# Spectral layer with a feed-forward gate: the second chunk transposed by DMA behind six tiles of w1, and each of these tiles scaled alone

## The chip, the cores and the metric

The kernel runs on one core of a Trainium2 chip. The core's engines work side by side, each through its own list of instructions in order: TensorE (PE in the profile: matmuls, and transposes as matmuls with an identity), VectorE (DVE), ScalarE (ACT), GpSimd (POOL) and SyncE (SP, which here only issues DMAs). They wait for one another by semaphores. Tiles stand in SBUF (128 partitions); matmuls write PSUM. The metric is the device time of one execution in microseconds (us); lower is better.

## What is computed

```python
def reference(A_x, A_w_r, A_w_i, B_x, B_w1, B_w2):
    x = A_x                                   # 1 x 2048 x 1024
    xn = _layernorm(x, axis=-1)
    X = rfft2(xn) * (w_r + 1j * w_i)          # over the last two axes
    s = irfft2(X, s=(2048, 1024))
    h = silu(einsum("bsd,df->bsf", xn, B_w1)) # B_w1: 1024 x 3584
    g = silu(einsum("bsf,fd->bsd", h, B_w2))  # B_w2: 3584 x 1024
    return x + s * g
```

## The kernel before

All matmuls take fp16. A float32 operand is scaled by a power of two and split into a high half (rounded to fp16) and a low half (the rest), and a product is three passes: high by high, high by low, low by high.

*Rows.* The 2048 rows stand in four chunks c = 0 to 3 of 512, each in four parts p of 128. `ln_gen(c)` normalises a chunk: statistics of a part on VectorE (L701 to 704), three small steps on POOL (L706 to 708), the normalisation on ScalarE (L709). Chunks 0 and 1 are then transposed on TensorE into `tp` (L718), ScalarE rounds the high half out of PSUM (L722, tile xnT) and VectorE takes the low half (L726). Chunks 2 and 3 (`TURNED`) are normalised into `xp` (two buffers), ScalarE takes the high half into `xs` (L687), VectorE the low half (L680), and both are transposed into xnT by DMAs on SP (L673), two per part. `xs` is one tile with room for a whole chunk (tag V, one buffer): the next chunk's `xs` may be written only when all DMA transposes of the one before have been read out.

*w1.* It is used in 28 tiles f of 128 columns. Of each: load (L271, SP), maximum of the absolute values per row (L274, VectorE), a column sum by one small matmul with ones (L258, TensorE, tile `s`), a chain of four small steps on VectorE that makes a power of two (`e`, `r`, `rs`; L279 to 282), the high half on ScalarE (L251), the low half on VectorE (L254). In the start two tiles share one column sum and one chain.

*First layer.* Product (c, f), `mm1`, is 24 matmuls (eight blocks d of the inner dimension by three passes) into one of four PSUM banks `pa`. For the first product the eight high-by-high matmuls come first; in the others the three passes of a block stand together. ScalarE evacuates it with silu into `h32` (L465), one tile for two f and two chunks, with two buffers. When its four parts are there, `hidden` forms sums and differences for the second layer, which is done with seven instead of eight block products: `hr` on VectorE (L494, L495), then high halves on ScalarE (`hosum`, `hoone`, L251), low halves on VectorE (L254), and seven stores to DRAM on SP (`hd_...`, L488). `hosum` and `hoone` have one buffer each: the next pair's high half waits until the stores of the one before have landed.

*Transforms.* `fa_mat` (L782 to 784) transforms a part of a chunk along the columns, 24 matmuls with 128 columns; ScalarE takes it out (L791, L792) and VectorE does the butterflies (L802 to 847). Later stages give s; `iu` and `ub` belong to the inverse transform, far behind.

*Order.* The program records instructions in a hand-written order; each engine executes its part of that list. The loop over `order` records product after product, and between products it takes steps ("slots") from two queues of generators: `bg` (normalisation, transforms) and `wq` (w1 tiles). `defer` puts DMA issues some steps later. Before the first product a list `WARM` alternates steps of the queues with spins, matmuls on ones whose result is not used (L1465). `FILL` names products with a transform block ahead of them; `EXTRA` names places with one more `wq` step.

## Time and profile before

| | us |
|---|---|
| median of three runs | 1235.21 (1234.19 to 1236.31) |
| the profiled execution | 1235.84 |
| its span | 1234.1 |
| TensorE busy in it | 1220.7 |
| VectorE / ScalarE / POOL busy | 999.0 / 467.6 / 117.3 |

The profile was taken in one execution. Its span runs from the first to the last instruction on the engines; the time of the same execution is 1.7 us longer. Rows name engine, line, output and inputs by the program's names without their numbers (pa for pa0_3), and give shapes as partitions by elements. In a timeline the first two columns are start and duration in us; brackets show idle time of that engine before, and what ended it. In a group's row stand busy time in all and nanoseconds of one, then idle time before. In a waits row stand total, count and longest. A row of windows has the stretch, its length, busy time of PE, PEld (weight loads), DVE, ACT and POOL with counts, the granted TensorE clock (1.00 is full speed), the DMA engines' share, and GB/s.

### The profile page before, as it was taken

What the parts mean: (1) busy time and instruction counts of PE and PEld (TensorE: products, weight loads), DVE (VectorE), ACT (ScalarE), POOL (GpSimd) and SP (SyncE); (2) the same over time, 40 slices, a digit from 0 to 9 for tenths busy, and PEclk for the clock granted to TensorE, in tenths of its full rate; (3) what the DMA queues carried; (4) which work ended last, traced back from release to release, by engine and by line L of the source; (5) the groups of instructions that cost most, each with busy time, mean ns of one, the idle gap of its engine ahead of it and who ended that gap; (6) DMA issues with size and microseconds to landing.
All of it is one profiled execution on the core that took longest, in us unless ns stands there. A gap on an engine that the chain in (4) does not pass through costs nothing.

```text
span 1234.1 us, 19097 instructions
## 1 busy us (share of the span) xinstructions
PE 1220.7 (99%) x7033; PEld 625.2 (51%) x7033; DVE 999.0 (81%) x1970; ACT 467.6 (38%) x614; POOL 117.3 (10%) x245
## 2 busy tenths in 40 slices
PE   8999999999999999999999999999999999999998
PEld 5545445444544454445545555554455555555545
DVE  7687988899798898896969899985186678798886
ACT  4865344333554565444433222122032222243212
POOL 2330000001000000010001121114111111000000
PEclk9999999999999999999999999999999999999999
DMA  7487476655758898759898999997989999998576
GB/s 253 134 172 187 135 224 201 185 152 161 223 172 237 276 283 242 217 177 279 207 283 224 283 259 198 276 256 246 293 207 278 286 289 331 315 332 325 200 261 260
DMA packets 271102, 293.67 MB, mean 238 GB/s; under 512 B 40096, under 2 KB 198816, under 8 KB 270624
## 3 DMA queue, kind: packets, MB, share of 16 engines
q1 hardware_dynamic: 250992, 233.66, 65.7%
q10 hardware_dynamic: 15984, 51.45, 12.0%
q0 software_dynamic: 4032, 7.34, 3.5%
q8 instruction: 55, 0.90, 0.3%
q14 instruction: 39, 0.32, 0.1%
HBM read 185.95 MB, written 102.25 MB: 234 GB/s over the span
## 4 chain that ended last, share of the span: by engine, by line
PE 75%; DVE 11%; DMA 9%; issue 2%; ACT 1%; SPq 0%; POOL 0%; DVEq 0%; ACTq 0%; POOLq 0%
PE pa L456 45%; PE pb L539 8%; PE pb L541 8%; PE pb L540 8%; DVE Z L1055 2%; DMA wq<-in_A_w_i_dram 2%; DMA sd<-s 2%; PE id L1294 2%; DMA zd<-zq 1%; DMA ht<-hd_sum_d 1%; DVE T L1020 1%; DVE w L254 1%; PE iu L1204 1%; ACT xp L709 1%; PE iu L1212 1%
## 5 line engine op out<-in xcount | busy, mean ns | idle before, releaser
L456 PE MATMUL pa<-xnT,w 128*128 128x512 f16 x2688 | 585.2, 379 | 1.1 <-ACT w L251 0.7
L456 PEld LDWEIGHTS <-w 128*128 128x128 f16 x2688 | 262.2, 98 | 311.6 <-DVE w L254 1.3
L539 PE MATMUL pb<-w,ht 128*128 128x512 f16 (+2 forms) x812 | 300.4, 372 | 0.0
L540 PE MATMUL pb<-w,ht 128*128 128x512 f16 (+2 forms) x812 | 300.4, 372 | 0.0
L541 PE MATMUL pb<-w,ht 128*128 128x512 f16 (+2 forms) x812 | 300.3, 372 | 0.0
L541 PEld LDWEIGHTS <-ht 128*128 128x128 f16 x812 | 79.4, 98 | 91.0
L539 PEld LDWEIGHTS <-ht 128*128 128x128 f16 x812 | 79.5, 98 | 86.7
L540 PEld LDWEIGHTS <-ht 128*128 128x128 f16 x812 | 79.4, 98 | 86.7
L465 ACT ACTIVATE h<-pa,s 128x512 f32<-128x512 f32 x112 | 75.5, 678 | 122.9 <-PE pa L456 111.0
L251 ACT ACTIVATE w<-jr,sc 128x512 f16<-128x512 f32 x98 | 68.1, 713 | 77.8 <-PE pb L541 22.1
L254 DVE SCALAR_TENSOR_TENSOR w<-jr,sc,w 128x512 f16<-128x512 f32 x98 | 71.1, 744 | 2.1 <-ACT w L251 2.1
L254 DVE SCALAR_TENSOR_TENSOR hoone<-h,hs,hoone 128x2048 f16<-128x2048 f32 x28 | 65.6, 2344 | 7.9 <-ACT hoone L251 7.9
L251 ACT ACTIVATE hoone<-h,hs 128x2048 f16<-128x2048 f32 x28 | 56.0, 1998 | 36.5 <-DVE h L499 24.3
L251 ACT ACTIVATE hosum<-hr,hs 128x1536 f16<-128x1536 f32 x28 | 44.1, 1574 | 64.1 <-DVE hr L495 26.8
L981 ACT ACTIVATE zq<-Z,zs 128x1024 f16<-128x1024 f32 x16 | 18.4, 1149 | 103.9 <-DVE Z L1055 57.0
L494 DVE TENSOR_TENSOR hr<-h 128x1024 f32<-128x1024 f32 x28 | 34.2, 1221 | 24.4 <-ACT h L465 24.3
L254 DVE SCALAR_TENSOR_TENSOR hosum<-hr,hs,hosum 128x1536 f16<-128x1536 f32 x28 | 50.7, 1812 | 3.1 <-ACT hosum L251 3.1
L251 ACT ACTIVATE w<-w1r,rs 128x1024 f16<-128x1024 f32 x28 | 31.9, 1144 | 47.0 <-DVE w L254 31.8
L274 DVE TENSOR_REDUCE m<-w1r 128x1 f32<-128x1024 f32 x28 | 33.8, 1210 | 16.1 <-DMA w1r<-in_B_w_dram 16.1
L632 ACT ACTIVATE pl<-pl,c 128x512 f32<-128x512 f32 (+2 forms) x28 | 17.6, 657 | 70.1 <-DVE pl L608 41.6
L954 PE MATMUL fx<-vq,kq 128*128 128x256 f16 x192 | 43.2, 273 | 0.0
L955 PE MATMUL fx<-vq,kq 128*128 128x128 f16 x192 | 42.0, 219 | 0.0
(219 smaller groups left out, 1524.8 us busy)
## 6 DMA issues: line engine op xcount, KB each, us to landing
w1r<-in_B_w_dram SPq DMA_DIRECT2D x28, 512.0 KB, 6.2
hd_sum<-hosum SPq DMA_DIRECT2D x56, 256.0 KB, 2.9
hd_one<-hoone SPq DMA_DIRECT2D x56, 256.0 KB, 3.7
hd_dif<-hoone SPq DMA_DIRECT2D x56, 256.0 KB, 3.2
w2m<-in_B_w_dram SPq DMA_DIRECT2D x28, 512.0 KB, 5.2
ht<-hd_dif ACTq DMA_DIRECT2D x32, 448.0 KB, 6.3
jr<-in_B_w_dram SPq DMA_DIRECT2D x56, 256.0 KB, 6.8
ht<-hd_sum ACTq DMA_DIRECT2D x32, 448.0 KB, 6.4
```

The lines of the kernel that those rows point to most:

```text
L251: nc.scalar.activation(hi, raw, AF.Copy, scale=scale)
L254: nc.vector.scalar_tensor_tensor(lo, raw, scale, hi, op0=OP.mult, op1=OP.subtract)
L274: nc.vector.tensor_reduce(m1[:, i:i + 1], raw[i], axis=AX.XY, op=OP.max, apply_absolute_value=True)
L456: nc.tensor.matmul(ps, w[:, wh, d], xt[:, xh, d], start=(n == 0), stop=(n == 23))
L465: nc.scalar.activation(hq[:, 2 * (c % 2) + f % 2], ps, AF.Silu, scale=s1[:, f:f + 1])
L494: tt(sums[:, 0:2], hq[:, 0::2], hq[:, 1::2], op=OP.subtract)
L539: nc.tensor.matmul(ps, hh[:, 0], w[:, 0], start=first, stop=False)
L540: nc.tensor.matmul(ps, hh[:, 0], w[:, 1], start=False, stop=False)
L541: nc.tensor.matmul(ps, hh[:, 1], w[:, 0], start=False, stop=last)
L954: nc.tensor.matmul(o, k[:, c, kh, 1], v[:, c, vh], start=(n == 0), stop=False)
L955: nc.tensor.matmul(ps[:, c, 0], k[:, c, kh, 2], v[:, c, vh, 128:256], start=False, stop=False)
L1055: eng.tensor_tensor(Z[:, ns, pos], x0[:, :, ls], x1[:, :, ls], op=o_)
```

## The change

The order of the first twelve products becomes chunk 0 with f = 0 to 5, then chunk 1 with f = 0 to 5; before it was chunk 0 and 1 with f = 0 to 3, then both with 4 and 5. Chunk 1 is no longer transposed on TensorE: a new generator `entering` normalises it into `xp`, splits it and transposes it by DMA, as chunks 2 and 3 are; 32 transposes on TensorE go and eight on SP come. The first six tiles of w1 are scaled one by one (a sum and chain each), in a list of 24 steps; the high half of tile 0 is made on VectorE, and tile 1's maximum on ScalarE as a sum over |w| (`AF.Abs` with `accum_out`). Tiles 4 and 5 are loaded earlier, the next chunk's x later. In products with f up to 5 and c up to 1 all high-by-high matmuls come first. During the first six products, steps of the queues are recorded inside a product, after its 8th and 16th matmul and after its end (`ENTRY`: w and b are steps of the queues, f and e a transform block and its evacuation). Products (0, 4) and (0, 5) are evacuated into a tile `h32_early` and copied into their `h32` tile when (1, 4) is evacuated. The spins become 61 from 71. A line number of before moves by 1 to 30 in the changed file.

```diff
@@ -19,13 +19,14 @@
 S, D, F, DF = 2048, 1024, 3584, 513
 NFT = F // 128
 NP = NFT // 2
-WARM = [35, 8, 0, 8, 0, 8, 12, 0, 0, 0, 0]
+WARM = ("", 35), ("b", 10), ("w", 0), ("b", 0), ("w", 8), ("w", 0), ("b", 8), ("w", 0), ("b", 0), ("w", 0)
 LEAD, PAUSE, LAST, EARLY = 1.0, -1, 6, 2
 IORDER = (1, 3, 0, 2)
 SUMMED = (4, 5)
 TURNED = (2, 3)
-FILL = ((1, 0), (3, 0))
-EXTRA = (4, 5, 6, 7, 20, 22, 24)
+FILL = ((1, 0),)
+EXTRA = (20, 22, 24)
+ENTRY = ("wwbb|w|w", "ww|bbwb|", "fww|b|wbbwwb", "wbwb||w", "wbwbww|b|b", "be|b|bb")
 
 
 
@@ -300,28 +301,32 @@
         for i in range(4):
             load(i)
         yield 0
-        maxi(0)
-        yield 0
-        maxi(1)
-        yield 0
-        scales(0, 2)
-        yield 0
-        split(0)
-        yield 0
-        rest(0)
-        yield 0
-        split(1)
-        rest(1)
-        maxi(2)
-        maxi(3)
-        yield 0
-        scales(2, 2)
-        split(2)
-        rest(2)
-        yield 2
-        split(3)
-        rest(3)
-        yield 2
+        def whole(i):
+
+            if i == 0:
+                new[0] = fp.tile([128, 2, 8, 128], F16, name="w1_0", tag="w1", bufs=7)
+                nc.vector.tensor_single_scalar(new[0][:, 0], raw[0], rs[:, 0:1], op=OP.mult)
+            else:
+                split(i)
+            if i in (1, 2):
+                load(i + 3)
+
+        def bound(i):
+
+            if i == 1:
+                junk = A["p"].tile([128, 8, 128], F16, name="w1abs", tag="junk", bufs=1)
+                nc.scalar.activation(junk, raw[1], AF.Abs, accum_out=m1[:, 1:2])
+            else:
+                maxi(i)
+
+        def scale(i):
+            scales(i, 1)
+
+        steps = {"m": bound, "s": scale, "h": whole, "l": rest}
+        for k in "m0 s0 h0 m1 l0 s1 h1 m2 l1 s2 h2 m3 l2 s3 h3 l3 m4 s4 h4 m5 l4 s5 h5 l5".split():
+            steps[k[0]](int(k[1]))
+            yield 0
+
         def ahead(i):
 
             if i < NFT and i not in raw and i - len(used1) <= 4:
@@ -329,7 +334,7 @@
                 load(i + 1)
 
         last = None
-        for i in range(4, NFT, 2):
+        for i in range(6, NFT, 2):
             while i not in raw:
                 ahead(i)
                 yield 0
@@ -446,21 +451,30 @@
 
     done2, ready2, chunks = [0], [-1], [0]
 
-    def mm1(c, f):
+    def mm1(c, f, between={}):
         ps = pf.tile([128, 512], F32, name=f"pa{c}_{f}", tag="ff")
         w, xt = w1t[f], xnT[c]
         terms = [(d, wh, xh) for wh, xh in ((0, 0), (0, 1), (1, 0)) for d in range(8)]
-        if c + f:
+        if f > 5 or c > 1:
             terms.sort(key=lambda k: k[0])
         for n, (d, wh, xh) in enumerate(terms):
+            if n in between:
+                between[n]()
             nc.tensor.matmul(ps, w[:, wh, d], xt[:, xh, d], start=(n == 0), stop=(n == 23))
         if c == 3:
             used1.add(f)
         q, g = f // 2, c // 2
 
         def evac():
+            if (q, c) == (2, 0):
+                if f % 2 == 0:
+                    h32["early"] = A["p"].tile([128, 2, 512], F32, name="h32_early", tag="Ro", bufs=1)
+                nc.scalar.activation(h32["early"][:, f % 2], ps, AF.Silu, scale=s1[:, f:f + 1])
+                return None
             if (q, g) not in h32:
                 h32[q, g] = H["p"].tile([128, 4, 512], F32, name=f"h32_{q}_{g}", tag="h32", bufs=2)
+                if (q, c) == (2, 1):
+                    nc.scalar.activation(h32[q, g][:, 0:2], h32.pop("early"), AF.Copy)
             hq = h32[q, g]
             nc.scalar.activation(hq[:, 2 * (c % 2) + f % 2], ps, AF.Silu, scale=s1[:, f:f + 1])
             if c % 2 and f % 2:
@@ -692,6 +706,35 @@
                     stats(p)
             yield 2.5
 
+    def entering(c, stats, norm):
+
+        ap = A["p"]
+        split = ap.tile([128, 4, 2, 8, 128], F16, name=f"xs{c}", tag="V", bufs=1)
+        xn = {}
+
+        def plain(p):
+            xn[p] = ap.tile([128, 8, 128], F32, name=f"xp{c}_{p}", tag="Rs", bufs=2)
+            norm[p](xn[p].rearrange("s d1 d0 -> s d0 d1"), A["x"][c, p].rearrange("s (d0 d1) -> s d0 d1", d1=8))
+            A["x"].pop((c, p))
+            defer(1, lambda: load_x(c + 1, p))
+
+        def hi(p):
+            nc.scalar.activation(split[:, p, 0], xn[p], AF.Copy)
+
+        def turn(p, h):
+            nc.sync.dma_start_transpose(
+                xnT[c][:, h, :, p * 128:(p + 1) * 128], split[:, p, h].rearrange("s d1 d0 -> s (d1 d0)"))
+
+        def lo(p):
+            turn(p, 0)
+            nc.vector.tensor_tensor(split[:, p, 1], xn.pop(p), split[:, p, 0], op=OP.subtract)
+            turn(p, 1)
+
+        steps = {"s": stats, "n": plain, "h": hi, "l": lo}
+        for k in "s0 n0 h0 s1 l0 n1 h1 s2 l1 n2 s3 h2 l2 n3 h3 l3".split():
+            steps[k[0]](int(k[1]))
+            yield 0
+
     def ln_gen(c):
         ap = A["p"]
 
@@ -751,27 +794,7 @@
             lo(3)
             yield 0
             return
-        if c in TURNED:
-            yield from turned(c, stats, norm)
-            return
-        for i in range(4):
-            pair = range(2 * (i % 2), 2 * (i % 2) + 2)
-            for p in pair:
-                if i < 2:
-                    stats(p)
-                else:
-                    trans(p)
-                    if c < 3:
-                        load_x(c + 1, p)
-            if i < 2:
-                yield 2.5
-                for p in pair:
-                    norm[p]()
-                continue
-            for fn in (hi, lo):
-                for p in pair:
-                    fn(p)
-            yield 2.5
+        yield from (turned if c in TURNED else entering)(c, stats, norm)
 
     psa, l0 = {}, {}
 
@@ -1477,10 +1500,10 @@
         slot(wq)
         ln = [add(bg, ln_gen(0)), None, None, None]
         nc.gpsimd.memset(mhalf, -0.5)
-        spin(WARM[0])
-        for k, q in enumerate((bg, wq, bg, wq, bg, wq, wq, bg, wq, wq)):
-            slot(q)
-            spin(WARM[1 + k])
+        for k, n in WARM:
+            if k:
+                slot(wq if k == "w" else bg)
+            spin(n)
         for i in range(4):
             load_x(1, i)
             if i == 1:
@@ -1490,7 +1513,14 @@
         for c in range(4):
             add(bg, fd_gen(c))
 
-        order = [(c, f) for fs in ((0, 1, 2, 3), (4, 5)) for c in range(2) for f in fs]
+        def do(steps):
+            for k in steps:
+                if k in "fe":
+                    (fa_mat if k == "f" else fa_evac)(0, 0)
+                else:
+                    slot(wq if k == "w" else bg)
+
+        order = [(c, f) for c in range(2) for f in range(6)]
         order += [(2, 0), (2, 1), (2, 2), (3, 0), (3, 1), (2, 3), (3, 2), (3, 3), (2, 4), (2, 5), (3, 4), (3, 5)]
         order += [(c, f + i) for f in range(6, NFT - LAST, 2) for c in range(4) for i in range(2)]
         order += [(2 * g + c, f + i) for g in range(2) for f in range(NFT - LAST, NFT, 2) for c in range(2) for i in range(2)]
@@ -1526,20 +1556,20 @@
             while f not in w1t:
                 slot(wq)
             if (c, f) in FILL:
-                fa_mat(0, FILL.index((c, f)))
-                fa_evac(0, FILL.index((c, f)))
+                fa_mat(0, 1)
+                fa_evac(0, 1)
+            if n < len(ENTRY):
+                enter = [lambda k=k: do(k) for k in ENTRY[n].split("|")]
+                ev = mm1(c, f, {8: enter[0], 16: enter[1]})
+                settle()
+                enter[2]()
+                fresh_ev[0] = ev
+                tick()
+                continue
             ev = mm1(c, f)
             if left == 0:
                 for j, k in ((2, 0), (2, 1), (3, 0)):
                     load_h(0, j, k, nc.sync)
-            if n < 4:
-                slot(wq)
-                for _ in range((2, 0, 1, 1)[f]):
-                    slot(bg)
-                settle()
-                fresh_ev[0] = ev
-                tick()
-                continue
             after(ev)
             if n in EXTRA or left < 4 * LAST and (NFT - 3 not in w1t or left < 20 and not w1j.done) or left < 2 * LAST and (left % 2 or left < 8):
                 slot(wq)
```

How this moves instructions is shown at three places. First VectorE, around the maximum of w1 tile 4 (`m1` from `w1r4`), whose column sum TensorE needs for `s1_4`. Before:

```order
L704 BN_AGGR mv1_3_523<-st1_3_520 128x2
L254 SCALAR_TENSOR_TENSOR w1_3_554<-w1r3_258,rs1_224,w1_3_554 128x1024
L726 TENSOR_TENSOR xnT1_490<-tp1_0_590,xnT1_490 128x8x128
L726 TENSOR_TENSOR xnT1_490<-tp1_1_601,xnT1_490 128x8x128
L274 TENSOR_REDUCE m1_222<-w1r4_584 128x1
L726 TENSOR_TENSOR xnT1_490<-tp1_2_643,xnT1_490 128x8x128
```

After, on VectorE at the same tile:

```order
L280 TENSOR_SCALAR e1_221<-s1_3_577 128x1
L281 TENSOR_SCALAR e1_221<-e1_221 128x1
L282 RECIPROCAL r1_223<-e1_221 128x1
L283 TENSOR_SCALAR rs1_224<-r1_223 128x1
L287 TENSOR_TENSOR ep_226<-e1_221 128x1
L288 TENSOR_TENSOR hs_227<-r1_223 128x1
L255 SCALAR_TENSOR_TENSOR w1_3_587<-w1r3_258,rs1_224,w1_3_587 128x1024
L744 BN_STATS st1_2_610<-x1_2_430 128x6
L745 BN_STATS st1_2_610<-x1_2_430 128x6
L747 BN_AGGR mv1_2_613<-st1_2_610 128x2
L275 TENSOR_REDUCE m1_222<-w1r4_455 128x1
L280 TENSOR_SCALAR e1_221<-s1_4_620 128x1
```

The maximum now stands behind tile 3's chain and low half and part 2's statistics, and on TensorE the sum of tile 4 stands between products (0, 2) and (0, 3); before it stood between (1, 1) and (1, 2), with the maximum two products earlier.

Second ScalarE, where the first pair of tiles is split (`hosum_0_0_0`, `hoone_0_0_0`) and chunk 3 is normalised. Before:

```order
L251 ACTIVATE hosum_0_0_0_892<-hr0_0_849,hs_227 128x12x128
L465 ACTIVATE h32_1_0_669<-pa1_2_823,s1_225 128x512
L251 ACTIVATE hoone_0_0_0_942<-h32_0_0_557,hs_227 128x16x128
L465 ACTIVATE h32_1_0_669<-pa1_3_867,s1_225 128x512
L251 ACTIVATE hosum_0_1_0_978<-hr1_0_946,hs_227 128x12x128
L465 ACTIVATE h32_2_0_981<-pa0_4_917,s1_225 128x512
L709 ACTIVATE xp3_0_987<-x3_0_797,v3_0_903 128x128x8
L687 ACTIVATE xs3_897<-xp3_0_987 128x1024
```

After, from the first part of chunk 3 on ScalarE:

```order
L701 ACTIVATE xs3_910<-xp3_1_961 128x1024
L252 ACTIVATE hosum_0_0_0_1007<-hr0_0_955,hs_227 128x12x128
L479 ACTIVATE h32_1_0_671<-pa1_2_929,s1_225 128x512
L752 ACTIVATE xp3_2_1017<-x3_2_818,v3_2_969 128x128x8
L701 ACTIVATE xs3_910<-xp3_2_1017 128x1024
L752 ACTIVATE xp3_3_1020<-x3_3_820,v3_3_978 128x128x8
L701 ACTIVATE xs3_910<-xp3_3_1020 128x1024
L252 ACTIVATE hoone_0_0_0_1048<-h32_0_0_540,hs_227 128x16x128
L479 ACTIVATE h32_1_0_671<-pa1_3_982,s1_225 128x512
L252 ACTIVATE hosum_0_1_0_1090<-hr1_0_1052,hs_227 128x12x128
L477 ACTIVATE h32_2_0_1093<-h32_early_776 128x1024
L479 ACTIVATE h32_2_0_1093<-pa1_4_1023,s1_225 128x512
```

The whole of chunk 3's normalisation is now ahead of the first `hoone` on ScalarE; before all of it came behind that, and half of it behind the second one.

Third SP, with the loads of x (chunks 2 and 3) and the DMA transposes (x4 is two parts). Before:

```order
L660 DMA x3_0_797<-in_A_x_dram 128x1024
L660 DMA x3_1_799<-in_A_x_dram 128x1024
L673 DMA_TRANSPOSE xnT2_671<-xs2_672 128x8x128 x4
L660 DMA x3_2_852<-in_A_x_dram 128x1024
L660 DMA x3_3_854<-in_A_x_dram 128x1024
L673 DMA_TRANSPOSE xnT2_671<-xs2_672 128x8x128 x4
L488 DMA hd_sum_0_0_96<-hosum_0_0_0_892 512x1x256
```

After, on SP:

```order
L725 DMA_TRANSPOSE xnT1_457<-xs1_458 128x8x128 x2
L687 DMA_TRANSPOSE xnT2_748<-xs2_749 128x8x128 x4
L674 DMA x3_0_814<-in_A_x_dram 128x1024
L674 DMA x3_1_816<-in_A_x_dram 128x1024
L674 DMA x3_2_818<-in_A_x_dram 128x1024
L674 DMA x3_3_820<-in_A_x_dram 128x1024
L687 DMA_TRANSPOSE xnT2_748<-xs2_749 128x8x128 x4
L687 DMA_TRANSPOSE xnT3_909<-xs3_910 128x8x128 x4
```

All four loads of chunk 3 now stand ahead of chunk 2's last four transposes, and four transposes of chunk 3 follow directly.

## The prediction

> **What bounds the kernel now.** I read the page first (engines, then the chain that ended last):

> ```profile
> span 1234.1 us, 19097 instructions
> PE 1220.7 (99%) x7033; PEld 625.2 (51%) x7033; DVE 999.0 (81%) x1970; ACT 467.6 (38%) x614; POOL 117.3 (10%) x245
> PE 75%; DVE 11%; DMA 9%; issue 2%; ACT 1%; SPq 0%; POOL 0%; DVEq 0%; ACTq 0%; POOLq 0%
> ```

> TensorE is busy 99% of the span. So only two things change the time: work taken from TensorE, and stretches in which TensorE stands. I therefore read its waits, from after its first spins to the end, and then its timeline to 72 us (start, duration, line, in brackets the idle time before):

> ```profile
> PE tp L718 <- ACT x L709: 3.0, 3, 2.0
> PE iu L1212 <- DVE ub L1221: 1.7, 1, 1.7
> ```

> ```profile
> 17.02 0.28 PE L258 MATMUL s<-m,ones 128*128 128x2 f32 x2
> ...
> 19.34 5.35 PE L456 MATMUL pa<-xnT,w 128*128 128x512 f16 x24 [0.71 <-ACT w L251]
> 24.53 0.28 PE L258 MATMUL s<-m,ones 128*128 128x2 f32 x2
> 24.67 10.52 PE L456 MATMUL pa<-xnT,w 128*128 128x512 f16 x48
> 35.03 1.94 PE L718 MATMUL tp<-ident,x 128*128 128x128 f32 x16
> 36.80 5.34 PE L456 MATMUL pa<-xnT,w 128*128 128x512 f16 x24
> 41.98 1.95 PE L718 MATMUL tp<-ident,x 128*128 128x128 f32 x16
> 45.41 0.22 PE L782 MATMUL fa<-cas,xnT 128*128 128x128 f16 x1 [1.47 <-DVE xnT L726]
> ...
> 68.59 3.63 PE L456 MATMUL pa<-xnT,w 128*128 128x512 f16 x16 [0.40 <-DVE w L254]
> ```

> The first product starts at 19.34. From there a product takes 5.19 us by starts (24.67 minus 19.34, less 0.14 for the sum between). Everything the change touches lies before about 125 us, and TensorE's waits there after 19.34 are 1.47 and 0.40: little is to be had beside the work removed, and any new stand is paid in full.

> **The change, part by part: what it gains.** *Start.* In ScalarE's timeline:

> ```profile
> 16.34 1.02 ACT L722 ACTIVATE xnT<-tp 128x1024 f16<-128x1024 f32 x1 [0.56 <-PE tp L718]
> ...
> 18.14 2.19 ACT L251 ACTIVATE w<-w1r,rs 128x1024 f16<-128x1024 f32 x2 [0.77 <-DVE rs L282]
> ```

> Before, the first product waits for tile 0's high half, scaled on ScalarE after the pair's sum. With tile 0 scaled alone its sum comes a maximum (1.2) earlier, and the high half moves to VectorE, where no row of this shape stands; bounds are a half of the 1.21 of a reduce and the 1.27 of L254 below, and I take 1.2. By either it ends by about 17.0, so the last high part of chunk 0 (16.34 + 1.02) is what is left: the product starts at 17.4, a gain of 1.9. The ten spins fewer lie in that wait and count nothing more.

> *Transposes of chunk 1.* The two groups on TensorE go: 36.80 - 35.03 = 1.77, and 45.41 - 41.98 = 3.43 with its wait. The wait of 0.40 for tile 4's low half goes too, since those tiles are now split earlier. Gains together 1.9 + 1.77 + 3.43 + 0.40 = 7.5.

> **What it costs.** *Sums.* Seventeen column sums instead of fourteen, at 0.14 each (24.53 to 24.67): 0.4.

> *A sum that stands.* Tile 4's sum is now between the third and fourth product of chunk 0, and its maximum stands on VectorE behind the low half of tile 3 and the statistics of part 2. VectorE's groups, by form, 16 to 125 us (count, busy, mean ns):

> ```profile
> L680 DVE TENSOR_TENSOR xs<-xp,xs 128x1024 f16<-128x1024 f32 x8 | 9.7, 1219 | 6.0 <-ACT xs L687 6.0
> L702 DVE BATCH_NORM_STATS2 st<-x 128x6 f32<-128x512 f32 x12 | 8.1, 676 | 0.0
> L254 DVE SCALAR_TENSOR_TENSOR w<-w1r,rs,w 128x1024 f16<-128x1024 f32 x6 | 7.6, 1274 | 1.9 <-ACT w L251 1.9
> L274 DVE TENSOR_REDUCE m<-w1r 128x1 f32<-128x1024 f32 x6 | 7.1, 1203 | 0.0
> L254 DVE SCALAR_TENSOR_TENSOR hoone<-h,hs,hoone 128x2048 f16<-128x2048 f32 x3 | 7.0, 2347 | 0.7 <-ACT hoone L251 0.7
> L494 DVE TENSOR_TENSOR hr<-h 128x1024 f32<-128x1024 f32 x4 | 4.9, 1224 | 7.9 <-ACT h L465 7.8
> L495 DVE TENSOR_TENSOR hr<-h 128x512 f32<-128x512 f32 x4 | 2.7, 684 | 0.0
> L704 DVE BATCH_NORM_AGGREGATE mv<-st 128x2 f32<-128x12 f32 x12 | 2.5, 209 | 1.2
> ```

> Tile 3's sum runs after two products, eight matmuls of the third (1.7), the block of fa (1.3, 45.41 to 46.74) and two sums: 17.4 + 10.4 + 1.7 + 1.3 + 0.2 = 31.0. TensorE is then ready for tile 4's sum after sixteen matmuls, at 34.6. But from tile 3's sum lead: sum and scale 1.1 (17.02 to 18.14), high half 1.1 (2.19 for two), low 1.27, statistics 2 x 0.68 + 0.21, maximum 1.20: 31.0 + 6.3 = 37.3. Neither end depends on the start. TensorE stands 2.6. With roundings in the other terms I carry 2.5; bounds 1.5 (high half early in ScalarE's row) and 3.5. So at the end of chunk 1 the kernel is 7.5 - 0.4 - 2.5 = 4.6 us ahead.

> *Chunks 2 and 3.* Here the time goes back. ScalarE's groups, by form, 16 to 125 us; then of the transposes, the loads of x and the stores of hoone on SP their durations and times to landing:

> ```profile
> L709 ACT ACTIVATE xp<-x,v 128x1024 f32<-128x1024 f32 x8 | 17.3, 2162 | 0.8 <-POOL v L708 0.8
> L465 ACT ACTIVATE h<-pa,s 128x512 f32<-128x512 f32 x18 | 12.1, 677 | 9.4 <-PE pa L456 6.6 <-DVE hoone L254 2.8
> L687 ACT ACTIVATE xs<-xp 128x1024 f16<-128x1024 f32 x8 | 8.5, 1057 | 0.3
> L251 ACT ACTIVATE hosum<-hr,hs 128x1536 f16<-128x1536 f32 x4 | 6.3, 1572 | 8.7 <-DMA hd_sum_d<-hosum 5.9 <-DVE hr L495 2.8
> L251 ACT ACTIVATE hoone<-h,hs 128x2048 f16<-128x2048 f32 x3 | 6.0, 1989 | 0.0
> ```

> ```profile
> L673 SPq DMA_TRANSPOSE xnT<-xs x16: 1237/1351/2360, 55.1 to 102.0; - x16
> ...
> DMA to landing us min/median/max: 3.1/4.0/5.8
> ```

> ```profile
> DMA to landing us min/median/max: 3.7/4.5/5.2
> ```

> ```profile
> 79.78 0.51 SPq L488 DMA_DIRECT2D hd_one<-hoone  x1
> ...
> 81.73 0.67 SPq L488 DMA_DIRECT2D hd_one<-hoone  x1
> ```

> ```profile
> DMA to landing us min/median/max: 2.6/3.0/4.4
> ```

> Chunk 2's norms run on ScalarE from about 54 to 66.9, four times 2.16 + 1.06 = 12.9. On SP all four loads of chunk 3 now go, from 63.3, ahead of chunk 2's last four transposes; before, two went ahead of four. With 512 KB each at the rate of the full start (window below), they land 1.6 us apart, from 63.3 + 4.2 to 72.3; the transposes behind them, 256 KB each, then land between 0.8 (that rate) and 1.35 (SP's own step) apart. I take 1.05: the last lands at 76.5. If they do not queue behind the loads, they are issued to 70.4 and land by 74.4; the far end is 77.7.

> ```profile
> 2.00:19.34 17.34, 13.40 (x102) 10.82 (x100) 13.21 (x25) 10.05 (x12) 4.52 (x14) 1.00 1.06 330
> ...
> 95.00:125.00 30.00, 30.00 (x194) 15.83 (x193) 24.77 (x68) 15.36 (x19) 0.23 (x2) 1.00 0.69 170
> ```

> [...]

> ScalarE's first high half of chunk 3 goes into the one buffer that those transposes read, so it waits from 72.8 to 76.5 (3.7), and behind it wait all evacuations. In order follow xs, xp, xs, hosum, h, xp, xs, xp, xs, hoone, h = 4 x 1.06 + 3 x 2.16 + 1.57 + 1.99 + 2 x 0.68 = 15.6, less small overlaps, to 91.9. Then VectorE: hr 1.22 + 0.68, two lows 2.44, hoone's low 2.35: 98.4. Only now is an h32 buffer free (two of them): the copy of the early tile (1.1, as the 1.06 of L687) and one evacuation, 0.68: product (2,2) can start at 100.2. When would TensorE be ready?

> ```profile
> 100.67 5.34 PE L456 MATMUL pa<-xnT,w 128*128 128x512 f16 x24
> ```

> That is the same product before. Now it is 4.6 earlier, but one fa block (1.3) is ahead that came later: 97.4. TensorE stands **2.8**.

> The stores of hoone stand on SP behind four transposes and go at 99.0; they took 1.95 + 3.0 to 4.4 = 5.0 to 6.4 from the first issue to the last landing, I take 6.0: 105.0. The next hoone has the same buffer, so it ends at 107.0, and the evacuation behind it at 107.7; TensorE, ready at 106.8, stands **0.9**. VectorE then has hr 1.9, a fa butterfly 3.7 (below) and hoone's low 2.35, to 115.7; evacuation of (2,0) 116.4, TensorE stands **3.4**. Stores to 121.2, hoone and evacuation to 123.9: **2.1**. Together 9.2.

> ```profile
> 101.43 0.16 DVE L802 TENSOR_TENSOR L<-L,tws 128x8 f32<-128x8 f32 x1
> ...
> 104.89 0.29 DVE L820 TENSOR_TENSOR Q<-DS 128x130 f32<-128x130 f32 x1
> ```

> *After that.* VectorE was busy 24.77 of 30.00 us (95 to 125), so its backlog also reaches the low half of tile 7, at about 167: bounds 0 and its own 1.27, I take 1.0. The wait of 1.7 for ub at 1061 us stays; two FFN products change places there, bounds -1.7 and +3.

> **Sum.** -4.6 + 9.2 + 1.0 = +5.6 on the profiled execution's 1235.84, so 1241.4. The median of the runs is 0.63 below that execution: 1240.8.

> **Rivals.** *Transposes early.* If chunk 2's last transposes land by 73, ScalarE does not wait its 3.7 us: the first stand (2.8) and the second (0.9) go, the others keep 5.5: -4.6 + 5.5 + 1.0 = +1.9, 1237.1. For it: 4.0 is the median landing; against: that median is with two loads ahead at most.

> *Faster.* VectorE's low of the first hoone ends by 95.6 rather than 98.4, and the stores are not held behind transposes. Then nothing stands in 95 to 125, as in the window row above, where TensorE is busy 30.00 of 30.00: -4.6 alone, 1230.6. It decides at 95.6 + 1.8 = 97.4, TensorE's ready time. Against: ScalarE's order by itself needs 15.6 after the first xs. A version of it is that chunk 3 is late, but the tight stores only cost half: still above 1235.

> [...]

> *It doesn't do what it says.* If the first product still waits for tile 0, 1.9 is lost: 1242.7. The chain leaves 0.4 us of room, so I give it no chance of its own.

> **How the numbers follow.** Main case 0.66 (own range 1238 to 1244, from the bounds of the two landings and the sum that stands); slow clock 0.08; transposes early 0.13; faster 0.13. About 2.5 us (0.2%) is what a measurement of this kernel tells from no change, so transposes early counts as same: faster 0.13, same 0.13, slower 0.74. The range 1233 to 1246 leaves out most of the faster case and a few in a hundred above, where a second sum stands as well.

> **What would show it.** Right: first product at 17.4; no tp group after 19 us; one stand of about 2.5 before a sum at 35 to 37; ScalarE idle about 3.7 before an xs at 73 to 76; four stands of TensorE between 95 and 125 with ScalarE's h as releaser. Wrong: a full TensorE from 95 to 125, or xs waiting for nothing, or a granted clock under 1.00 behind a stand.

## The result, and the profile after

The changed kernel takes 1245.9 us (median of four runs, 1244.49 to 1246.98); the kernel before takes 1234.7. The ratio is 1.0069 (95% interval 1.0042 to 1.0096): slower by 11.2 us, where the forecast of 1240.8 was 5.6 more. The time lies above the main case's own range (1238 to 1244) and 0.1 below the upper end of the stated one (1246).

In what follows, a stand is a stretch in which TensorE waits, and a low clock is a granted clock under 1.00. First the page of the changed kernel: span, engines, the granted clock in 40 slices, and the chain that ended last.

```profile
span 1244.9 us, 19060 instructions
PE 1221.7 (98%) x6997; PEld 622.1 (50%) x6997; DVE 1000.6 (80%) x1982; ACT 471.3 (38%) x616; POOL 109.2 (9%) x248
PEclk9998999999999999999999999999999999999999
PE 70%; DVE 13%; DMA 8%; SPq 3%; issue 3%; ACT 3%; POOL 0%; DVEq 0%; ACTq 0%; POOLq 0%
```

TensorE has less to do (36 instructions fewer) and is yet busy 1.0 us longer. The clock row says why: the fourth slice (93 to 124 us) is no longer at full speed. Next TensorE's waits behind its first spins, and the rows of its timeline at the places that the prediction named:

```profile
PE pa L463 <- ACT h L479: 7.4, 4, 2.8
PE tp L761 <- ACT x L752: 2.9, 3, 2.5
PE s L259 <- DVE m L275: 2.6, 1, 2.6
PE iu L1235 <- DVE ub L1244: 1.9, 1, 1.9
PE pa L463 <- DVE w L255: 1.5, 1, 1.5
PE pb L553 <- DMA ht<-hd_dif: 1.0, 1, 1.0
```

```profile
17.26 1.89 PE L463 MATMUL pa<-xnT,w 128*128 128x512 f16 x8 [0.24 <-ACT xnT L765]
...
37.35 0.35 PE L259 MATMUL s<-m,ones 128*128 128x1 f32 x2 [2.58 <-DVE m L275]
```

```profile
95.23 5.34 PE L463 MATMUL pa<-xnT,w 128*128 128x512 f16 x24 [1.20 <-ACT h L479]
103.35 6.88 PE L463 MATMUL pa<-xnT,w 128*128 128x512 f16 x24 [2.78 <-ACT h L479]
111.40 5.34 PE L463 MATMUL pa<-xnT,w 128*128 128x512 f16 x24
119.00 7.03 PE L463 MATMUL pa<-xnT,w 128*128 128x512 f16 x24 [2.26 <-ACT h L479]
```

The start is there (17.26 instead of 19.34), and the stand at tile 4's sum, and four stands between 94 and 128 us (the fourth is 1.17 and ends at 127.20). Two products behind a stand take 6.88 and 7.03 us where others take 5.34. The windows behind three of the stands (the clock is the third figure from the right):

```profile
37.35:42.00 4.65, 4.65 (x15) 1.91 (x16) 4.08 (x8) 3.49 (x3) 0.36 (x2) 0.63 0.58 109
103.35:106.80 3.45, 3.45 (x9) 1.26 (x9) 1.08 (x1) 0.00 (x0) 0.00 (x0) 0.55 1.03 278
119.00:123.50 4.50, 4.50 (x14) 1.68 (x14) 4.36 (x19) 0.00 (x0) 0.00 (x0) 0.63 0.86 234
```

So after each of the stands of 2.58, 2.78 and 2.26 us the clock fell, for some eight matmuls. By the spacing of matmuls, 0.43 instead of 0.22 us, that cost 1.69, 1.53 and 1.69 us. Behind the stands of 1.20 and 1.17 it stayed at 1.00, and also behind one of 2.48 us at the start (6.48 to 8.96, the longest of the tp row above). So length alone does not decide; the stands by design below come back to this.

Last, ScalarE in the same stretch, and the row of the first hoone before:

```profile
75.81 2.18 ACT L752 ACTIVATE xp<-x,v 128x1024 f32<-128x1024 f32 x1 [4.36 <-POOL v L751]
80.18 1.06 ACT L701 ACTIVATE xs<-xp 128x1024 f16<-128x1024 f32 x1 [2.19 <-DMA xnT<-xs]
...
92.62 1.99 ACT L252 ACTIVATE hoone<-h,hs 128x2048 f16<-128x2048 f32 x1
...
101.66 1.06 ACT L477 ACTIVATE h<-h_early 128x1024 f32<-128x1024 f32 x1 [3.02 <-DVE hoone L255]
...
107.78 2.00 ACT L252 ACTIVATE hoone<-h,hs 128x2048 f16<-128x2048 f32 x1 [4.49 <-DMA hd_one<-hoone]
```

```profile
71.66 1.99 ACT L251 ACTIVATE hoone<-h,hs 128x2048 f16<-128x2048 f32 x1
```

The first hoone runs at 92.6; before it ran at 71.7. Its low half frees the h32 buffer, and its stores free the buffer of the next hoone.

### The profile page after: what moved, and what is told of

The parts are those of the page before. It is cut to its first block, busy times and chain, and to the rows that moved or that the text cites. A ratio compares the mean times of both kernels' runs of the same rounds, so it can differ in the third digit from the quotient of the medians.

```text
span 1244.9 us, 19060 instructions
## 1 busy us (share of the span) xinstructions
PE 1221.7 (98%) x6997; PEld 622.1 (50%) x6997; DVE 1000.6 (80%) x1982; ACT 471.3 (38%) x616; POOL 109.2 (9%) x248
## 4 chain that ended last, share of the span: by engine, by line
PE 70%; DVE 13%; DMA 8%; SPq 3%; issue 3%; ACT 3%; POOL 0%; DVEq 0%; ACTq 0%; POOLq 0%
PE pa L463 33%; PE pb L553 10%; PE pb L555 10%; PE pb L554 10%; SPq L502 2%; PE id L1317 2%; DMA jr<-in_B_w_dram 2%; DMA zd<-zq 1%; ACT xp L752 1%; DVE Z L1078 1%; DMA hd_one<-hoone 1%; DVE w L255 1%; DVE hoone L255 1%; DMA x<-in_A_x_dram 1%; PE iu L1227 1%
```

## The experiments

Three questions were open: whether the low clock is caused by the stands, what holds the first hoone back, and what the parts of the change are worth once the stands are gone. The runs come from several chips, so each time stands with its ratio to the kernel before on the same chip. *Theory A* is that each long stand brings a low clock, and that ScalarE's order causes the stands behind 95 us; B, C and D are named in the expectations.

**Tile 4's maximum earlier (e1).** One swap in the list of steps:

```diff
-... s3 h3 l3 m4 s4 h4 ...
+... s3 h3 m4 l3 s4 h4 ...
```

> The changed kernel with one swap in its list of steps: tile 4's maximum ahead of tile 3's low half. Theory A (every stand of TensorE of over about 2.2 us is followed by some 3.4 us at half clock, which cost 1.6 each in the changed kernel): the stand of 2.6 before tile 4's sum goes, and with it the low clock from 38 to 42 us (1.7): 4.3 less, 1241.6 from 1245.9. Theory B (the low clock comes at its time, whatever TensorE did just before): only the 2.6 goes, 1243.3, and the granted clock near 38 to 42 stays under 1.

1242.39 us, ratio 1.0052 (1.0034 to 1.0069). The stand is gone, and so is the low clock at that time:

```profile
38.00:42.00 4.00, 4.00 (x20) 1.82 (x19) 3.90 (x6) 3.68 (x4) 1.44 (x3) 1.00 0.79 140
```

That is A. The time alone would not decide it: the median fell by 3.5 (by the ratios 2.1), between A's 4.3 and B's 2.6. In the profiled execution the four later stands were 0.3 longer in all (7.7), and the wait for ht (the second layer's operand, read back from DRAM) at 755 us was 0.6 longer.

**Spins in the stand (e2).** The work waits as before, but TensorE turns over matmuls on ones:

```diff
         def scale(i):
+            if i == 4:
+                cover(20)   # a new helper: 20 matmuls on ones, 256 columns each
             scales(i, 1)
```

> The changed kernel with 20 spins (matmuls on ones) ahead of tile 4's column sum: the useful work waits as long as before, but TensorE is not idle. Theory A: the granted clock stays at 1.00 behind it, 1.7 less: 1244.2. Theory B: no change, 1245.9; if the spins end later than the maximum, up to 0.5 more.

1244.74 us, ratio 1.0076 (1.0055 to 1.0098). The medians differ from the changed kernel's by 1.2 in the expected direction; the ratios do not tell the two apart. The trace does: the spins take 2.35 us, 0.31 of the stand is left, and the clock stays up.

```profile
38.00:42.00 4.00, 3.69 (x23) 1.97 (x21) 3.42 (x8) 2.32 (x3) 1.25 (x4) 1.00 0.35 68
```

So from 38 to 42 us the clock reads 1.00, where in the changed kernel it read 0.63 (37.35 to 42.00) behind 2.58 us of idle: what TensorE did decided, not the moment. B falls. In this execution a low clock fell on the start instead (11.93 to 15.34 us, behind a stand of 2.44), and the first product began at 19.20.

**Hidden layer ahead of chunk 3 (e3).** No bg step behind product (1,1):

```diff
+            hold[0] = hold[0] or n in (7,)
             after(ev)
```

> The changed kernel with no step of the bg queue behind the eighth product (1,1), so that hosum and hoone of the first pair stand ahead of chunk 3's normalisation on ScalarE. Theory A (ScalarE's order holds the first hoone back): the four stands from 95 to 128 us (7.4), their two low clocks (3.2) and the wait for tile 7 at 171 (1.5) go, 12.1 less: 1233.8. Theory C (the wait of ScalarE for chunk 2's DMA transposes sets the rest, whatever stands ahead of it): chunk 3 then comes as late or later, a new stand of 3 or more before (3,0), and the time is 1240 or more.

1233.28 us, ratio 0.9976 (0.9963 to 0.9989): 12.6 us less than the changed kernel by the medians, 11.5 by the ratios, and faster than before. ScalarE, and TensorE's waits from 5 us on:

```profile
73.42 1.58 ACT L252 ACTIVATE hosum<-hr,hs 128x1536 f16<-128x1536 f32 x1 [1.90 <-DVE hr L509]
...
79.82 1.06 ACT L701 ACTIVATE xs<-xp 128x1024 f16<-128x1024 f32 x1
...
83.95 1.99 ACT L252 ACTIVATE hoone<-h,hs 128x2048 f16<-128x2048 f32 x1
...
97.46 1.04 ACT L477 ACTIVATE h<-h_early 128x1024 f32<-128x1024 f32 x1
```

```profile
...
PE s L259 <- DVE m L275: 2.6, 1, 2.6
PE pa L463 <- ACT h L479: 1.2, 1, 1.2
...
PE pa L463 <- DMA xnT<-xs: 0.2, 1, 0.2
```

hosum runs at 73.4 instead of 84.3, hoone at 84.0 instead of 92.6. The order came out only half as the expectation had it: hosum stands ahead of all of chunk 3, hoone ahead of its last two parts. ScalarE's first high half of chunk 3 no longer waits, though the transposes that it needs landed at 79.6, hardly sooner than before the edit (80.0): ScalarE comes to it later. Of the four stands 1.25 is left, and the waits for tile 7 and for ht are gone. C asked for a new stand of 3 before (3,0); it is 0.2. The only low clock left is the one behind tile 4's sum (0.62 from 37.36 to 41.86).

**Loads of x behind the transposes (e4).** The step of the prediction that started the chain:

```diff
                     turn(p, 1)
+                    if c < 3:
+                        load_x(c + 1, p)
...
-                    if c < 3:
-                        defer(1, lambda p=p: load_x(c + 1, p))
```

> The changed kernel with each load of chunk 3's x behind the two DMA transposes of the same part of chunk 2 on SP, not all four ahead of the last four. The prediction's step (the loads ahead of the transposes make ScalarE wait): ScalarE's wait of 2.2 before xs3 goes, and 2 to 3 us of the first stands; with one low clock less 1.6 more: 1241.5 to 1243.5. Theory C: all four stands shrink with it, 1236 to 1239. If the loads do not hold the transposes, nothing changes: 1245.9, or more because chunk 3's x comes later.

1244.5 us, ratio 1.0067 (1.0045 to 1.0089): no difference to the changed kernel that could be told. ScalarE's wait did not go:

```profile
79.97 1.06 ACT L703 ACTIVATE xs<-xp 128x1024 f16<-128x1024 f32 x1 [2.92 <-DMA xnT<-xs]
```

The high half starts 0.2 us sooner than with the loads ahead. The last transpose landed at 79.9 (80.0 before this edit), with the loads now between the transposes. So this edit moved the loads but did not remove the wait, and what the wait alone is worth it does not show. TensorE's four stands sum to 7.5.

**Both edits (e5).** Maximum earlier and hidden layer first:

> The changed kernel with both edits: tile 4's maximum ahead of tile 3's low half, and no bg step behind the eighth product. Theory A: from 1233.3 (the second edit alone) the stand of 2.6 at 37 us and the low clock behind it (1.7) go: 1229.0, some 6 faster than before. Theory D (what bounds chunk 3, its loads, transposes and ScalarE, does not move with TensorE): TensorE comes 4.3 earlier to the same waits, which were 1.25 at 99 and 0.2 at 106 us, and they grow by up to 4.3: 1230 to 1233.

1231.29 us (ten runs), ratio 0.9951 (0.9934 to 0.9967): 5.6 us faster than before by the medians, or 0.5%. This version beats both kernels, as e3 does by less. The waits from 19 us on, and product (2,2):

```profile
PE iu L1235 <- DVE ub L1244: 1.8, 1, 1.8
PE pa L463 <- ACT h L479: 1.3, 1, 1.3
```

```profile
94.47 5.34 PE L463 MATMUL pa<-xnT,w 128*128 128x512 f16 x24 [1.32 <-ACT h L479]
```

The remaining stand is 1.32 at 94.5, where it was 1.25 at 99.1 with the second edit alone. It did not grow though TensorE came 4.7 us earlier: what feeds it moves with TensorE, so D falls at this place, although the time lies in the range that D gave. The gain over the second edit alone is 0.0025 of 1236, or 3.1 us by the ratios, where 4.3 was expected. The granted clock of each run goes with its time: five of the six runs at 0.999 or 1.000 took 1229.2 to 1230.4 (A said 1229.0), the four at 0.996 to 0.998 took 1232.2 to 1235.5.

**A shared sum again (e6).** From the kernel with both edits, tiles 0 and 1 go back to one sum:

```diff
-m0 s0 h0 m1 l0 s1 h1 ...   # scale(0): scales(0, 1)
+m0 m1 s0 h0 l0 s1 h1 ...   # scale(0): scales(0, 2); scale(1): nothing
```

> As the kernel with both edits, but tiles 0 and 1 share one column sum and one chain, as before the change (tile 0's high half stays on VectorE). The prediction's step (tile 0 alone lets the first product start at 17.4): it starts at 20 to 21, TensorE stands before the sum and before the product, 2 to 3.5 more than the kernel with both edits. If the start is covered by something later (chunk 1 or 3 late anyway), less than 1 more.

1233.73 us, ratio 0.9977 (0.9961 to 0.9993), 2.4 more. TensorE's timeline:

```profile
16.43 0.38 PE L259 MATMUL s<-m,ones 128*128 128x2 f32 x2 [1.79 <-ACT w1abs L318]
...
19.60 2.76 PE L466 MATMUL pa<-xnT,w 128*128 128x512 f16 x12 [0.93 <-DVE w L308]
```

The first product starts at 19.60; in the kernel with both edits it starts at 17.05. The 2.55 at the start comes out at the end as 2.4 by the medians, 3.2 by the ratios.

**Chunk 1 on TensorE again (e7).** In the kernel with both edits, the same places of the order, but transposes on TensorE and no DMA transposes of chunk 1 (shortened; `trans`, `hi_` and `lo_` are the old steps of `ln_gen`):

```diff
         def hi(p):
-            nc.scalar.activation(split[:, p, 0], xn[p], AF.Copy)
+            trans(p)        # eight transposes on TensorE
+            defer(1, lambda: load_x(c + 1, p))
+            hi_(p)          # high half out of PSUM, as in chunk 0
...
+        lo = lo_
```

> As the kernel with both edits, but chunk 1 is transposed on TensorE (32 transposes, halves taken from PSUM by ScalarE and VectorE) in the same places of the order, and the eight DMA transposes are gone. The prediction's step (transposes on TensorE cost 1.77 per eight pairs): 2 x 1.77 = 3.5 more. If the DMA transposes hold back chunks 2 and 3 (theory D), part of it is given back: 0 to 2 more.

1233.05 us, ratio 0.9963 (0.9948 to 0.9979): 1.8 more by the medians, within the second expectation (0 to 2), but the intervals of the ratios overlap. Among the runs at a clock of 0.999 or 1.000 alone it is 2.9 (seven runs against six), near the first (3.5), so the times do not choose. In the traces product (2,2) starts 3.1 later (97.59 instead of 94.47), but its stand is 0.30 instead of 1.32: TensorE was ready 4.1 later, and 1.0 of that is given back there.

```profile
97.59 5.34 PE L463 MATMUL pa<-xnT,w 128*128 128x512 f16 x24 [0.30 <-ACT h L479]
```

**Stands by design, first series (e8; the second series is e10).** The kernel before, with waits for small activations put into TensorE's list:

```diff
+        def probe(ps, k):            # behind product n, k from a table
+            for i in range(k):
+                nc.scalar.activation(probe_t.bitcast(F16)[:, 0:128], ps[:, 0:128], AF.Copy, scale=0.0)
...                                   # sp is a PSUM tile, junk is probe_t read as fp16
+            nc.tensor.matmul(sp[:, 0:128], junk[:, 0:128], junk[:, 0:128], start=True, stop=True)
```

> The kernel before with 14 stands put into it: behind every fifth product from the 31st on, TensorE waits for 2 to 10 small activations on ScalarE (five lengths, some 1 to 4 us of standing). Theory A (a stand of over 2.2 us is followed by 3.4 us at half clock): all stands over 2.2 us show it, none below, each costs 1.6 beside its length. Theory B (the clock does not answer to stands): none shows it. If it depends on where the stand falls in a window of fixed length, some stands of 2 to 3.4 us show it and some do not, and all over 3.4 do.

> The kernel before with 18 stands, behind every fourth product from the 31st on: 7, 9, 11 or 13 small activations, by the spacing of the first series (0.31 each) some 2.2, 2.8, 3.5 and 4.1 us. If the clock answers to a window of about 3.4 us that runs freely: of the 2.2 few or none, of the 2.8 about half, of the 3.5 and 4.1 nearly all are followed by a slow stretch, each costing 1.3 to 1.7. If it is a fixed length instead, one of the four lengths divides all that show it from all that don't.

The second expectation is that of a second series, with 18 longer stands. Together, by the granted clock in the 4.5 us behind each stand (low: 0.50 to 0.70; all others read 1.00):

| length of the stand, us | stands | followed by a low clock |
|---|---|---|
| 0.7 to 1.9 | 8 | 0 |
| 2.2 | 5 | 3 |
| 2.5 to 2.8 | 7 | 4 |
| 3.1 to 3.5 | 8 | 7 |
| 4.1 | 4 | 4 |

No length divides those with from those without. Two stands of the same 2.23 us in the second series show both answers, in TensorE's timeline and in the windows behind:

```profile
412.12 0.23 PE L1480 MATMUL spin<-probe 128*128 128x128 f16 x1 [2.23 <-ACT probe L1477]
412.19 2.39 PE L459 MATMUL pa<-xnT,w 128*128 128x512 f16 x7
```

```profile
520.25 0.23 PE L1480 MATMUL spin<-probe 128*128 128x128 f16 x1 [2.23 <-ACT probe L1477]
520.31 1.89 PE L459 MATMUL pa<-xnT,w 128*128 128x512 f16 x8
```

```profile
412.12:416.62 4.50, 4.50 (x14) 1.78 (x15) 3.76 (x12) 4.50 (x6) 0.00 (x0) 0.62 0.98 266
520.25:524.75 4.50, 4.50 (x22) 2.12 (x23) 2.60 (x3) 4.50 (x6) 0.00 (x0) 1.00 0.47 184
```

What divides them is in the traces too. Apart from the last microseconds of the kernel, every low stretch is 3.41 us long, or twice that, and within a trace all of them start whole multiples of 3.41 us apart: at 38.22, 103.08 and 120.14 in the changed kernel (19 and 5 such windows), and all sixteen of the second series, from 194.55 to 935.25, on one grid (217 windows). Here is that grid around the stand at 409.90 to 412.12, and then around the one at 518.02 to 520.25:

```profile
409.60:413.01 3.41, 1.19 (x7) 0.47 (x6) 3.41 (x16) 2.88 (x8) 0.00 (x0) 1.00 0.88 231
413.01:416.42 3.41, 3.41 (x9) 1.22 (x8) 2.70 (x5) 3.41 (x4) 0.00 (x0) 0.50 0.96 272
```

```profile
515.41:518.82 3.41, 2.61 (x13) 0.98 (x10) 3.35 (x17) 0.70 (x3) 0.00 (x0) 1.00 1.06 243
518.82:522.23 3.41, 1.98 (x10) 0.95 (x11) 0.11 (x1) 3.28 (x7) 0.00 (x0) 1.00 0.79 285
522.23:525.64 3.41, 3.41 (x19) 1.61 (x18) 3.24 (x5) 3.41 (x6) 0.00 (x0) 1.00 0.03 10
```

The first stand fell into one window (3.41 - 1.19 = 2.22 us idle), and the next window ran at 0.50. The second was cut by the grid into 0.80 and 1.43, and nothing followed. All twelve traces agree. Of their windows at full clock, the 26 in which TensorE idled 2.08 us or more were all followed by a low one. Of the 4288 in which it idled 1.97 or less, two were: one with transposes at the start of e2 (1.73) and one with matmuls of 8 and 24 columns at 931.8 in the second series (0.31); why these two were is not shown. Of the stands by design of 2.2 to 3.5 us, 14 of 20 were followed by a low clock and 6 were not, as the grid cut them. An estimate from these counts: if the grid cuts at random, and with a bound of 2.025, midway between 1.97 and 2.08, the chance for a stand of such a length L is (3.41 + L - 2 x 2.025) / 3.41, 0.46 at 2.2 and 0.78 at 3.3, near the 3 of 5 and 7 of 8 counted.

One low window cost 1.3 to 1.7 us where it passed over products alone. Behind three of the longer stands the clock stayed low for two windows (6.83 us), at a cost of 2.5 to 2.9. The times were 1270.17 and 1327.2 us (one run each), against 1236.92 for the kernel before: 33.3 and 90.3 more, of which the stands themselves are 26.8 and 56.1.

**All three edits (e9).** Both edits and the loads behind the transposes:

> The kernel with both edits, and each load of chunk 3's x behind the two DMA transposes of the same part of chunk 2. If chunk 2's transposes still hold ScalarE (theory D), the stand of 1.3 at 94 us goes and the ratio to before falls by 0.001 (1.3 us) to about 0.994. If not, as with the loads alone, nothing changes: ratio 0.995.

1230.39 us, ratio 0.9955 (0.9939 to 0.9971), the same as with both edits.

```profile
PE pa L463 <- ACT h L479: 1.2, 1, 1.2
```

The stand is 1.2 where it was 1.3. Where the loads stand on SP does not matter here either.

## Why the prediction was right, and where not

*Direction and place* were right: the gains of the start and the transposes came, and more than their sum was lost in stands of TensorE at the two places that were named. That the time fell inside the stated range was in part luck. The main case's own range ended at 1244, and its sum has no term for low clocks: no sum of the prediction gave 1245.9.

*Start*: 17.4 forecast, 17.26 measured; e6 shows that the single scaling is its cause, worth 2.4 to 2.6. *Transposes*: no group on TensorE after 19 us. Their worth was put at 3.5 plus the waits; e7 shows 1.8 to 2.9 at the end and 3.1 at product (2,2), since part of it is given back in a stand. *The sum that stands*: 2.6 from the chain of VectorE, with both ends right (TensorE ready at 34.77 for 34.6, the maximum done at 37.2 for 37.3), 2.58 measured, and e1 shows the cause. *The lead* of 4.6 at the end of chunk 1 can be checked at product (2,2): TensorE was ready at 103.35 - 2.78 = 100.57, which holds one fa block more than before (1.3), the stand of 1.20 and one low clock (1.69): without them 96.4, which is 4.3 ahead of the 100.67 before.

*Four stands*: 9.2 forecast, 1.20 + 2.78 + 2.26 + 1.17 = 7.4 measured, as the evacuations' wait, but at (2,1), (2,2), (3,1) and (2,3), not (3,0). That 2.78 stood at (2,2), as forecast, is luck: the product started at 103.35 for 100.2 and TensorE was ready at 100.57 for 97.4, both 3.2 later. (The terms from 91.9 to hoone's low half add up to 98.6, not 98.4.) *Tile 7*: 1.0 forecast, 1.48. So with its own terms the sum comes to -4.3 + 7.4 + 1.5 = +4.6, near the +5.6 forecast. The span grew by 10.8.

*The step that failed* is the one that made the slow clock a rival beside the main case, at 0.08, and not a term of its sum. The rows of the kernel before say of it only that an idle of 2.0 left the clock at 1.00; what length of stand brings a low clock, and at what cost, they do not show. So no run shows what the 0.08 stands on; in its place the runs showed that three stands of 2.26 to 2.78 us each brought a low clock of 3.41 us, at 1.5 to 1.7 us each and 4.9 in all. The idle of 2.0 said little: the grid of the kernel before cut it into windows with 1.29 and 0.87 of idle, and the windows that were followed by a low one, but for two, had 2.08 or more. The grid does not begin with the span: one of its windows begins 4.09 us from the start of the span in the changed kernel, and 4.62 in the kernel before. The waits for ht (1.0) and ub (0.2 more) make up the rest: 4.6 + 4.9 + 1.2 = 10.7 of 10.8.

*A cause that was named wrongly.* The loads of x ahead of the transposes were taken as the head of the chain (ScalarE waiting 3.7). Behind them SP was held 3.48 and 3.79 us in issuing the next two transposes, where most took 1.2 to 1.3, and the last landed at 80.0, beyond the far end of 77.7 that the prediction allowed for its 76.5. But ScalarE's wait for them was only 2.2, behind a longer one of 4.4 for statistics of chunk 3. e3 shows what carries the stands: with the loads in place and the last landing at 79.6, the order on ScalarE alone took 7.4 us of standing down to 1.25. e4 moved the loads without removing the wait, so what is left open is how much the 2.2 added. The prediction had that order in its sum of 15.6 us and still looked for the cause in the DMA queue. The rival "transposes early" was built on the same cause, and no run gave it.

*Rivals*: "faster" was to be decided by hoone's low half ending by 95.6; it ended at 101.6, and the kernel was slower. With the order of e3 it ended at 92.9, and the kernel was faster than before. It does not decide alone, though: (2,2) still stood 1.25 there, because the copy of the early tile (97.46) stood behind the last two parts of chunk 3 on ScalarE.

What stays open: why the expected 4.3 of e1 and of e5 over e3 came as 3.5 or 2.1 and 3.1. A low window is not met in every run, which can account for part of it: the four runs of e1 had a mean clock of 0.996 to 0.999, those of the changed kernel 0.995 or 0.996, and a single low window takes 0.0014 of it (half of 3.41 in some 1240 us). Of the 27 runs of the kernel before that go with e5 to e8, the eleven at a clock of 1.000 took 1233.9 to 1236.9 and the ten at 0.997 or 0.998 took 1237.8 to 1241.4; which stands were followed by a low clock in runs without a trace is not known. Whether the last 1.3 would go with a later place for chunk 3's last two parts, or with a second buffer for xs or hoone, was not tried.

## What to carry to other kernels

A stand of TensorE can cost more than its length: of the 24 stands by design of 2.2 us and more 18 were followed by a low clock, of the 8 of up to 1.9 none. Price the low window behind it (1.3 to 1.7 us here) as a term of the sum, times its chance. Where a stand cannot be removed, spins in it are worth a trial: in e2 2.35 us of them left the clock at 1.00. When prefetch work for a later stage moves forward in an engine's list, look at what it is put ahead of: here 12.9 us of normalisation stood ahead of the one split that frees the buffers. Before settling on a cause in a queue, move the suspect in the order, which took one line here. Compare runs at the same granted clock, where a kernel's runs differ in it.
